# Attention and a two-layer MLP in one kernel: the first batch's queries in two token halves, PSUM banks handed out by age

## The chip, the cores and the metric

The kernel runs on one core of a Trainium2 chip. A core has five engines that run side by side, each through its own queue in order: TensorE (PE, matmuls), VectorE (DVE), ScalarE (ACT), GpSimd (POOL) and SyncE (SP, which issues loads and stores). They meet through semaphores. The metric is the device time of one execution in microseconds; a row of the profile gives times in microseconds too, from the start of the span.

## The reference

Eight batches of twelve heads, 448 tokens and 64 features per head. Queries and keys are scaled to length one, scores are divided by tau = 0.1, softmax weights are applied to the values, and the heads' outputs stand side by side as 3584 rows of 768. Those go through two matrices with a hard swish in between.

```python
q_n = q / (np.linalg.norm(q, axis=-1, keepdims=True) + 1e-06)
k_n = k / (np.linalg.norm(k, axis=-1, keepdims=True) + 1e-06)
attn = softmax(np.matmul(q_n, k_n.transpose(0, 1, 3, 2)) / tau)
x = heads_side_by_side(np.matmul(attn, v))        # 3584 x 768
h = x @ w_in                                      # 3584 x 2048
out = (h * np.clip(h + 3.0, 0.0, 6.0) / 6.0) @ w_out
```

## The kernel before

**Tiling.** Heads are taken in pairs, six pairs to a batch, 48 in all; pair i belongs to batch i // 6. A pair of heads fills the 128 partitions, 64 features each. A query or key load (`load_qk`, an "item") brings the rows of two pairs; its squares are summed (`square`, `reduce`), turned into inverse lengths (`norms` on ACT, or `powers` and `reciprocals` with DVE), and multiplied in (`normalise`). In the first 14 items `transposes` turns the result on PE into PSUM, from where `copy_q`, `copy_k` and `copy_k3` bring it to SBUF; later items are turned by a transposing DMA.

**Scores and values.** `scores(i, g)` makes the scores of group g of pair i, with the keys on the partitions. Groups 0 to 2 hold 128 keys of each head, as two matmuls on the upper and lower half of the array; group 3 holds the last 64 keys of both heads. `exps` takes the exponential on ACT (softmax needs no maximum here, since the scores are bounded), `values` multiplies with the values, which carry a column of ones so that the sums come out as a 65th column, and `finish_values` divides on DVE. `back` (or a transposing DMA) turns the result into `xT`, the first layer's input, and `copy_x` brings it to SBUF.

**Layers.** `mm1_unit(b, fc)` is one of 16 units of the first layer for a batch: six matmuls of 448 columns, a Relu on ACT and one product on DVE. The second layer's units are `mm2_unit`, and `product_unit` for pairs of row blocks that share sums of weights (`weight_sums`, `g_sum`).

**Order.** Up to pair 18 (`FIRST`) the order of all work is written out by hand in `PLAN`, a list of words that `run` reads one by one; each word appends instructions to the queue of the engine that does it. From pair 18 on a loop (L1089) interleaves attention with the units that `TURNS` names, the same for every pair of its kind. The words:

| word | work | engine |
|---|---|---|
| LQ.j, LV.d, W | load of an item, of values, of a piece of the weights | SP, SP, POOL |
| SQ.j.e, RE.j, NO.d, NM.j.e | squares, sums, inverse lengths, scaling | e, DVE, ACT, e |
| TR.j, CQ.i.e, CK.i.e, CS.i.e | transposes and copies of queries and keys | PE, e, e, e |
| SC.i.g, EX.i.g, VA.i.g, FI.i | scores, exponentials, values, division | PE, ACT, PE, DVE |
| BK.i, CX.i.e, VC.i.e | transposes back, their copy, cast of values | PE, e, e |
| U, UA, UV | a unit's matmuls, its ACT step, its DVE step | PE, ACT, DVE |
| DP.n, D.n | n fillers: matmuls of zeros of 248 or 512 columns | PE |

(e is a, v or p for ACT, DVE or POOL.) The first rows of the plan of before:

```python
"LQ.1 DP.5 SQ.1.a.11.3 SQ.1.p.4.3 DP.1 SQ.1.a.0.4 LQ.0 SQ.0.p.8.6 DP.2 DP.4 LQ.3 LQ.2 SQ.1.v.7.4 RE.1.1",
"SQ.0.a.0.6 RE.1.0 NO.0.1 LQ.5 LQ.4 SQ.0.v.6.2 DP.6 SQ.3.a.0.7 NM.1.p.0 D.10 RE.0.1 DP.3 NM.1.p.1 RE.0.0 DP.8",
"NO.0.0 LV.0 DP.2 SQ.2.a.0.7 NM.0.p.0 RE.3 RE.2 NM.0.p.1 TR.1.Y DP.2 TR.0.Z CK.0.v DP.4 SQ.4.p.0.7 CQ.0.v",
"SQ.5.a.0.7 LQ.6 NO.1 LV.1 LQ.7 SC.0.0.0 SC.0.1.1 DP.5 DP.3 CQ.1.v EX.0.0 RE.5 RE.4 NM.3.p SC.0.2.0 CK.1.v",
```

The first unit (the first U) stands in its fifteenth row, after all of batch 0's values, pair 6's exponentials and most of pair 7's.

**PSUM.** Eight banks. While batch 0 runs, four hold scores two by two (`SC`, L1078), one exponential reading both, two (`PV`) the values, and `Y` and `Z` what else is turned. After batch 0 `open_ring` (L1020) makes a ring of six single banks in a fixed order of turns. `bank_of` notes at build time how many readers a bank still has; what runs on the chip is only the waits that follow from the order.

Of the kernel before, what the change touches and what calls it, by code (L numbers as in the profile page):

```python
# [18 lines left out]
ORDER = "1111111111111111111111111111112222222122"  # L19

PLAN = [
# [43 lines left out]
def kernel(  # L65
# [61 lines left out]
    def item(n):  # L127
# [4 lines left out]
        for c in range((NR + 2) * RAW, (NR + 2) * RAW + NV * VAL, VAL)  # L132
    ]
    NVX = 4
    vx = [const.tile([128, 8, D + 1], BF16, name=f"vx{i}", tag=f"vx{i}") for i in range(NVX)]
    raws = [item((i + 2) % NR) for i in range(NR)]

    def raw_before(j):
# [21 lines left out]
    def next_bank():  # L160
        ring_n[0] += 1
        return ring[(ring_n[0] - 1) % len(ring)]
# [1032 lines left out]
```

## Time and profile before

| what | value |
|---|---|
| median of 3 runs | 402.08 us (401.6 to 402.13) |
| span of the profiled execution | 399.5 us |
| PE busy | 391.4 us, 98% of the span |
| DVE, ACT, POOL busy | 291.1, 274.3, 235.9 us |
| granted clock of PE, mean | 0.999 |
| first unit of the first layer | 39.65 us |
| first score of the loop (pair 18) | 114.67 us |

The time of the profiled execution itself is not given, only its span from the first to the last instruction; the runs' median lies 2.6 us above that. Busy time is the union of an engine's instructions. For PE it runs from a matmul's start to the end of its latency, so that a short burst shows more busy time than the array was fed for, and the distance from one start to the next tells what a matmul costs.

### The profile page before, as it was taken

To read this page: it belongs to the slowest core of one execution; us is meant where nothing else is said; L and a number is where in the kernel's file an instruction comes from. 1 tells how busy PE (TensorE), PEld (TensorE's weight loads), DVE (VectorE), ACT (ScalarE), POOL (GpSimd) and SP (SyncE) were. 2 spreads that over 40 slices of the span, in tenths; PEclk is the share of its full clock that TensorE was granted. 3 is DMA by queue.
4 is the path that set the end of the run, shared out by engine and by line. 5 is a ranking of instruction groups with operands and counts; after the bars stand their busy time and mean duration, and the time that the engine had idled before them with its cause. 6 is when DMAs were issued, how large, how long until landed. Compare 5 with 4: busy or idle time off the path is not lost.

```text
span 399.5 us, 9623 instructions
## 1 busy us (share of the span) xinstructions
PE 391.4 (98%) x3673; PEld 230.9 (58%) x3673; DVE 291.1 (73%) x514; ACT 274.3 (69%) x627; POOL 235.9 (59%) x234
## 2 busy tenths in 40 slices
PE   7999999999999999999999999999999999999996
PEld 5656466555555556555555555555565556555563
DVE  6898988889878597766878775976766565645663
ACT  6899998886887676887776776767658655224230
POOL 7897229652853989579859829688396500400070
PEclk9999999999999999999999999999999999999999
DMA  8999987797987678795888386694953424230133
GB/s 292 291 226 252 240 188 206 149 172 193 222 201 171 159 193 183 174 231 152 196 178 230 81 203 158 155 198 136 193 125 75 103 48 67 46 74 21 31 71 97
DMA packets 92365, 63.73 MB, mean 160 GB/s; under 512 B 56096, under 2 KB 91552, under 8 KB 92320
## 3 DMA queue, kind: packets, MB, share of 16 engines
q1 hardware_dynamic: 87408, 56.45, 58.6%
q0 software_dynamic: 4512, 6.29, 9.3%
q8 instruction: 28, 0.46, 0.5%
q10 hardware_dynamic: 400, 0.39, 0.3%
q14 instruction: 17, 0.14, 0.1%
HBM read 45.61 MB, written 11.01 MB: 142 GB/s over the span
## 4 chain that ended last, share of the span: by engine, by line
PE 90%; ACT 5%; DMA 1%; DVE 1%; POOL 1%; issue 0%; SPq 0%; ACTq 0%
PE M L598 24%; PE M L794 19%; PE PV L486 11%; PE Y L598 6%; PE Z L598 6%; PE M L445 5%; PE Z L794 5%; PE Y L794 4%; ACT at L463 4%; PE Z L445 1%; PE Y L445 1%; PE M L874 1%; PE PV L1016 1%; DMA big<-in_q_dram 1%; POOL nrm L297 1%; PE Z L659 1%
## 5 line engine op out<-in xcount | busy, mean ns | idle before, releaser
L598 PE MATMUL M<-xT,w_in_sb 128*128 128x448 bf16 x522 | 110.7, 353 | 0.1
L598 PEld LDWEIGHTS <-w_in_sb 128*128 128x128 bf16 x768 | 72.0, 98 | 62.2 <-issue 1.9
L463 ACT ACTIVATE at<-M 128x448 bf16<-128x448 f32 x192 | 96.4, 569 | 16.7 <-PE M L445 15.7
L297 POOL TENSOR_TENSOR nrm<-big,r 128x896 bf16<-128x896 f32 (+1 forms) x46 | 77.1, 1680 | 27.8 <-ACT r L260 10.7
L229 POOL TENSOR_TENSOR big<-big 128x896 f32<-128x896 f32 (+3 forms) x41 | 60.8, 1488 | 16.6 <-DVE n L241 11.0
L620 DVE SCALAR_TENSOR_TENSOR gT<-u,M 128x448 bf16<-128x448 bf16 x76 | 46.2, 616 | 32.0 <-ACT u L614 31.8
L614 ACT ACTIVATE u<-M 128x448 bf16<-128x448 f32 x87 | 48.5, 560 | 28.3 <-PE M L598 27.9
L486 PEld LDWEIGHTS <-at 128*128 128x128 bf16 (+1 forms) x1536 | 53.0, 97 | 22.8 <-issue 14.4
L486 PE MATMUL PV<-vx,at 128*128 128x65 bf16 (+1 forms) x1536 | 62.3, 193 | 0.3 <-DVE on L507 0.2
L241 DVE TENSOR_REDUCE n<-big 128x14 f32<-128x896 f32 (+1 forms) x50 | 51.7, 1041 | 5.7 <-POOL big L229 3.9
L794 PEld LDWEIGHTS <-gT 128*128 128x128 bf16 x336 | 32.5, 98 | 23.3 <-issue 0.4
L823 POOL TENSOR_TENSOR big<-big 128x384 f32<-128x384 f32 x13 | 13.4, 1034 | 53.7 <-ACT big L842 53.5
L794 PE MATMUL M<-w_out_sb,gT 128*128 128x384 bf16 x224 | 40.2, 326 | 0.0
L794 PEld LDWEIGHTS <-gs 128*128 128x128 bf16 x280 | 27.0, 98 | 18.7 <-issue 0.5
L402 POOL COPY km<-tT 64x128 bf16<-64x128 bf16 x34 | 14.0, 413 | 34.7 <-PE M L445 9.7
L507 DVE TENSOR_TENSOR on<-PV,rc 128x512 bf16<-128x512 f32 x48 | 33.2, 691 | 1.7
L794 PE MATMUL M<-w_sum,gs 128*128 128x384 bf16 (+1 forms) x192 | 34.2, 323 | 0.0
L463 ACT ACTIVATE at<-Y 128x448 bf16<-128x448 f32 x52 | 29.6, 569 | 6.0 <-PE Z L445 5.9
L445 PE MATMUL M<-tT,kz 64*128 64x448 bf16 x169 | 31.1, 351 | 0.3 <-DVE gT L620 0.2
L463 ACT ACTIVATE at<-Z 128x448 bf16<-128x448 f32 x50 | 28.8, 576 | 0.4 <-PE M L445 0.4
L598 PE MATMUL Y<-xT,w_in_sb 128*128 128x448 bf16 x126 | 27.4, 353 | 0.0
L316 POOL CAST vx<-big 128x512 bf16<-128x512 f32 x36 | 24.1, 672 | 4.9 <-DMA big<-in_v_dram 4.9
(137 smaller groups left out, 563.1 us busy)
## 6 DMA issues: line engine op xcount, KB each, us to landing
big<-in_k_dram SPq DMA_DIRECT2D x24, 448.0 KB, 4.5
big<-in_q_dram SPq DMA_DIRECT2D x24, 448.0 KB, 4.2
out_dram<-o SPq DMA_DIRECT2D x107, 96.0 KB, 2.2
big<-in_v_dram SPq DMA_DIRECT2D x48, 128.0 KB, 4.2
big<-in_v_dram SPq DMA_DIRECT2D x48, 96.0 KB, 4.1
w_out_sb<-in_moe_w_out_dram POOLq DMA_DIRECT2D x4, 768.0 KB, 9.4
w_in_sb<-in_moe_w_in_dram POOLq DMA_DIRECT2D x4, 384.0 KB, 10.7
w_in_sb<-in_moe_w_in_dram POOLq DMA_DIRECT2D x2, 768.0 KB, 21.5
```

The costliest lines, as they stand in the source:

```text
L229: engines[e].tensor_tensor(out=o, in0=i, in1=i, op=ALU.mult)
L241: nc.vector.tensor_reduce(out=n2s[d % 2][:, j % 2, c], in_=sq[:, :, :, :].rearrange("p g c d -> p (g c) d")[:, c, :], axis=AX.X, op=ALU.add,)
L297: engines[e].tensor_tensor(out=nrm[:, :, g, :].rearrange("p c g d -> p g c d"), in0=raw_of[j][:, g, :, :], in1=rs[d % 2][3][:, j % 2, :] . ...
L316: (engines[e].copy if e == "a" else engines[e].tensor_copy)(out=o, in_=f)
L445: nc.tensor.matmul(o, ks, qt[rows], start=True, stop=True)
L463: nc.scalar.activation(out=o, in_=x, func=AF.Exp, scale=inv_tau)
L486: nc.tensor.matmul(pv_out(j, h), at[rows, n, q_cols(i // HP, j)], vt[rows, 3 + h if name == "M" else 5 * h + int(name[1]), :], start=(name ...
L507: nc.vector.tensor_tensor(out=on[:, :, :, :].rearrange("p j h d -> p h j d"), in0=pv4[:, :, :, 0:D], in1=rc[:, :, :].to_broadcast([128, 2, ...
L598: nc.tensor.matmul(ps[:, 0:S], w_in_sb[:, cc, fc * 128 : (fc + 1) * 128], x[:, cc, 0:S], start=(cc == 0), stop=(cc == CC - 1),)
L614: nc.scalar.activation(out=u[:, :], in_=ps[:, 0:S], func=AF.Relu, bias=0.5, scale=1.0 / 6.0)
L620: nc.vector.scalar_tensor_tensor(out=g[:, fc, c0 : c0 + S], in0=u[:, :], scalar=1.0, in1=ps[:, 0:S], op0=ALU.min, op1=ALU.mult,)
L794: nc.tensor.matmul(m, lhs[:, c, :], rhs[:, c, c0 : c0 + width], start=(base is None and c == 0), stop=(c == KC - 1), skip_group_check=True,)
```

## The change

**Halves.** Batch 0's 448 tokens are taken as 256 and 192 (`span_of`). For each pair and half, `half_scores(i, h, x)` makes groups 0 and 1 (x = 0) or 2 and 3 (x = 1) in two banks, `half_exps` reads each bank with one exponential of 512, 384, 256 or 192 columns, `half_values` adds up in one bank per half (two in turn, `half_pv`), `half_finish` divides, and `half_back` and `half_copy_x` bring the half to `xT`. In x = 1 group 3 goes into a bank that group 2 writes too, so PE waits for its own matmul first (`wait`). Words hS, hE, hV, hF, hB, hX name these. All 16 first-layer units of batch 0 run twice, on 256 columns (U.f) and on 192 (U.l); U.x are whole units of batch 1, U.s the second layer's. UA and UV name the unit they finish (UA.f3), so that they need not come in order.

**Buffers of batch 0.** Keys, queries and values of batch 0 get a buffer for each pair, laid into the tiles that later hold sums of weights (`kz_first`, `qT_first`, `vx_first`).

**PSUM.** The ring of six single banks is there from the start; `bank_of` gives the bank that has been free longest. The other two hold the halves' values, then `PV`.

**Constants.** The ones and zeros of the later value buffers are cleared by POOL; DVE clears those of the first batch's five in one piece and a sixth apart, and a column range of the six exponential buffers.

**Order.** `PLAN` is written anew (its first eleven rows stand below). Fillers: 68 of 248 columns in place of 79 and ten of 512. The code of the loop stays, but for the banks.

```diff
@@ PLAN
+    "LQ.1 SQ.1.a.7.4 LQ.0 LQ.3 SQ.1.v.11.3 RE.1.1 SQ.1.a.0.4 LQ.2 SQ.1.a.4.3 RE.1.0 SQ.0.a.8.6 SQ.0.p.0.6 NO.0.1",
+    "NM.1.p.0 NM.1.p.1 DP.55 TR.1 SQ.0.v.6.2 RE.0.1 RE.0.0 SQ.3.a.0.7 NO.0.0 NM.0.p.0 RE.3 LQ.5 NM.0.v.1 SQ.2.a.0.7",
+    "RE.2 CK.0.a SQ.5.a.0.7 LV.0 VC.0.p DP.8 TR.0 CQ.0.v CK.1.v VC.1.v LQ.6 DP.4 hS.0.1.0 W LQ.4 hS.0.1.1 NO.1",
+    "hE.0.1.0 NM.3.p hS.0.0.0 CQ.1.v hS.1.0.0 hE.0.1.1 LV.2 hV.0.1.0 hE.0.0.0 hS.0.0.1 W NM.2.p W hE.0.0.1 hS.1.1.0",
+    "hV.0.1.1 hE.1.0.0 RE.5 LV.1 TR.3 hS.1.0.1 DP.1 TR.2 SQ.4.v.0.7 hV.0.0.0 hV.0.0.1 RE.4 NO.2 hF.0.1 CK.3.v",
+    "hE.1.1.0 hV.1.0.0 hS.1.1.1 CQ.2.v LQ.7 CK.2.v hE.1.0.1 hS.2.0.0 CQ.3.v NM.5.p hE.1.1.1 W W W hF.0.0 hS.3.0.1",
+    "hE.2.0.0 hV.1.0.1 hE.3.0.1 VC.3.p hS.3.0.0 NM.4.v TR.4 TR.5 VC.2.p hF.1.0 hV.1.1.0 CQ.5.v hS.2.0.1 hV.1.1.1",
+    "CQ.4.v hE.3.0.0 CK.4.v hS.4.0.0 CK.5.v hS.5.0.0 hF.1.1 hV.2.0.0 hV.3.0.0 hE.2.0.1 hV.2.0.1 SQ.7.p.0.7 VC.4.v",
+    "hV.3.0.1 VC.5.p hB.0.0 hF.2.0 SQ.6.p.0.7 hE.4.0.0 hX.0.0.v hS.4.0.1 hF.3.0 hE.5.0.0 hV.4.0.0 hS.5.0.1 RE.7",
+    "hE.4.0.1 LQ.9 hE.5.0.1 hS.4.1.1 hE.4.1.1 hB.2.0 hX.2.0.v hV.4.0.1 hF.4.0 hV.5.0.0 hB.1.0 LQ.8 hX.1.0.v hB.3.0",
+    "hV.5.0.1 hS.4.1.0 LV.3 hX.3.0.a hS.3.1.1 hE.4.1.0 hF.5.0 hB.4.0 hX.4.0.v hE.3.1.1 hB.5.0 SQ.9.p.0.7 hX.5.0.v U.f",
...
-    PV = psum.tile([128, 2, 512], FP32, name="PV", tag="PV")
-    Y = psum.tile([128, 512], FP32, name="Y", tag="Y")
-    Z = psum.tile([128, 512], FP32, name="Z", tag="Z")
-    ring = []
+    ring = [psum.tile([128, 512], FP32, name=f"M{n}", tag=f"M{n}") for n in range(6)]
+    half_pv = [psum_h.tile([128, 512], FP32, name=f"H{n}", tag=f"H{n}") for n in range(2)]
...
     def next_bank():
-        ring_n[0] += 1
-        return ring[(ring_n[0] - 1) % len(ring)]
+        one = [n for n in range(6) if free(n)]
+        return ring[min(one, key=age)]
+    def release(key):
+        unread[key] -= 1
+        if not unread[key]:
+            ring_n[0] += 1
+            freed[key] = ring_n[0]
...
+    def half_scores(i, h, x):
+        kt, qt = score_operands(i, 0)
+        q0, w = span_of(h)
+        two, keys = zip(bank_of(1), bank_of(1))
+        for s in range(2):
+            if x and s:
+                break
+            for n in range(2):
+                rows = slice(64 * n, 64 * n + 64)
+                g = 2 * x + s
+                last = nc.tensor.matmul(two[n][:, 256 * s : 256 * s + w], kt[rows, 128 * g : 128 * g + 128],
+                                        qt[rows, q0 : q0 + w], start=True, stop=True, skip_group_check=True)
+                if n == 0:
+                    upper = last
+        if x:
+            for n in (1, 0):
+                rows = slice(64 * n, 64 * n + 64)
+                if n:
+                    wait = nc.tensor.nop(nofuse=True)
+                    tc.add_manual_dep(wait.ins, upper.ins.name, info, reason="one half of the array at a time in a bank")
+                nc.tensor.matmul(two[0][rows, 256 : 256 + w], kt[rows, KM : KM + SR], qt[rows, q0 : q0 + w],
+                                 start=True, stop=True, skip_group_check=True)
...
+    def half_exps(i, h, x):
...
+        for n, z in enumerate(two):
+            src, to = (t.rearrange("p (s n) -> p s n", n=256)[:, 0 : 2 - x * n, 0:w] for t in (z[:, :], at[:, n, :]))
+            nc.scalar.activation(out=to, in_=src, func=AF.Exp, scale=inv_tau)
...
+    def mm1_unit(b, fc, ends=None, h=None):
+        needs(*(("CX", i) if h is None else ("hCX", i, h) for i in range(b * HP, (b + 1) * HP)))
+        q0, w = (0, S) if h is None else span_of(h)
...
     def busy(n):
-        bank_of("Y", 0)
+        z = next_bank()
         for _ in range(n):
-            nc.tensor.matmul(Y[:, :], zeros[:, 0:128], zeros[:, :], start=True, stop=True)
+            nc.tensor.matmul(z[:, 0:248], zeros[:, 0:128], zeros[:, 0:248], start=True, stop=True)
...
-    for t in vx:
-        nc.vector.memset(t[:, :, D : D + 1], 1.0)
...
+    for t in (five, vx_first[5].rearrange("p (i c) d -> p i c d", i=1)):
+        nc.vector.memset(t[:, :, :, D : D + 1], 1.0)
...
+    for t in vx:
+        nc.gpsimd.memset(t[:, :, D : D + 1], 1.0)
...
+    for t in ats[2]:
+        nc.vector.memset(t[:, :, 192:256], 1.0)
```

More of the change, by code (lines that the diff above doesn't have):

```diff
@@ new lines, in half_exps @@
+    def half_exps(i, h, x):
+        at = ats[2][at_n[2] % len(ats[2])]
+        assert all(x is not at for x in at_of.values()) and (i, h, x) in sc_of
+        at_n[2] += 1
+        at_of[(i, h, x)] = at
+        w = span_of(h)[1]
+        two, keys = sc_of.pop((i, h, x))
+        for key in keys:
+            release(key)
+        for n, z in enumerate(two):
+            src, to = (t.rearrange("p (s n) -> p s n", n=256)[:, 0 : 2 - x * n, 0:w] for t in (z[:, :], at[:, n, :]))
+            nc.scalar.activation(out=to, in_=src, func=AF.Exp, scale=inv_tau)
@@ new lines, with half_values @@
+    pv_n, half_n = [0], [0]
+    pv_of, half_on, half_tiles = {}, {}, []
+    def half_values(i, h, x):
+        needs(("VC", i), ("hE", i, h, x))
+        if x == 0:
+            assert not pv_of.get(pv_n[0] % 2)
+            pv_of[i, h] = pv_n[0] % 2
+            pv_of[pv_n[0] % 2] = True
+            pv_n[0] += 1
+        else:
+            needs(("hV", i, h, 0))
+        bank = pv_of[i, h]
+        at = at_of.pop((i, h, x))
+        vt = vx_of(i)
+        parts = [(0, 0, 0), (0, 1, 1), (1, 0, 5), (1, 1, 6)] if x == 0 else [(0, 0, 2), (1, 0, 7), (0, 1, 3), (0, 1, 4)]
+        for y, (n, s, c) in enumerate(parts):
+            head = int(c > 3)
+            for j in range(2):
+                nc.tensor.matmul(
+                    half_pv[bank][:, (D + 1) * (2 * head + j) : (D + 1) * (2 * head + j + 1)],
+                    at[:, n, 256 * s + 128 * j : 256 * s + 128 * j + 128],
+                    vt[:, c, :],
+                    start=(x == 0 and y == 0 and j == 0),
+                    stop=(x == 1),
+                    skip_group_check=True,
+                )
+        if x:
+            issued.add(("hVA", i, h))
+            if ("hVA", i, 1 - h) in issued:
+                issued.update(("VA", i, g) for g in range(4))
@@ new lines, in half_back, with half_copy_x @@
+    def half_back(i, h):
+        needs(("hF", i, h))
+        z, key = bank_of(1)
+        z = z.bitcast(BF16)
+        z_of[-1 - i, h] = z, key
+        for j in range(2):
+            nc.tensor.transpose(z[:, 128 * j : 128 * j + 128], half_on[i, h][1][:, j, :, :], ident[:, :])
+    def half_copy_x(i, h, e="v"):
+        z, key = z_of.pop((-1 - i, h))
+        release(key)
+        q0, w = span_of(h)
+        copy(e, xT[0][:, i, q0 : q0 + w], z[:, 0:w].rearrange("p (t n) -> p t n", n=64))
+        issued.add(("hCX", i, h))
+        if ("hCX", i, 1 - h) in issued:
+            issued.update((("BK", i), ("CX", i)))
@@ L512, in finish_values, with back @@
         )
-    def back(i, bank=None):
-        z, key = bank_of(bank, 1)
-        if bank is not None:
-            z = z[:, :].bitcast(BF16)
+    def back(i):
+        needs(("FI", i))
+        z, key = bank_of(1)
         z_of[-1 - i] = z, key
```

276 lines of the change are left out of this document (178 added, 98 removed), and 72 rows, old and new, of the table PLAN.

## The prediction

> **What bounds the kernel now.** I read the page first: one engine, PE, is busy nearly throughout, and its clock is granted in full.
>
> ```profile
> span 399.5 us, 9623 instructions
> PE 391.4 (98%) x3673; PEld 230.9 (58%) x3673; DVE 291.1 (73%) x514; ACT 274.3 (69%) x627; POOL 235.9 (59%) x234
> ```
>
> The table by stretches comes next, cut at the first first-layer unit (39.65) and at the first score of the loop (114.67):
>
> ```profile
> 0.00:39.65 39.65, 35.82 (x447) 23.75 (x447) 32.69 (x82) 34.11 (x69) 32.75 (x45) 1.00 0.99 265
> 39.65:62.50 22.85, 22.57 (x244) 12.89 (x242) 19.87 (x37) 21.74 (x53) 7.65 (x6) 1.00 0.97 221
> 62.50:114.67 52.17, 52.09 (x504) 29.70 (x501) 44.33 (x76) 42.88 (x101) 30.99 (x32) 1.00 0.89 189
> 114.67:399.50 284.83, 280.88 (x2491) 164.59 (x2488) 194.23 (x322) 175.60 (x409) 164.56 (x153) 1.00 0.59 135
> ```
>
> From 39.65 on PE is full, so what counts is how much PE work stands there and when the full stretch begins. Ahead of 39.65 PE's 35.82 is not what it seems: it holds fillers and the tails of short bursts. PE's timeline and, for back-to-back prices, the chain of waits (there a piece runs to the next one's start) give the durations:
>
> ```profile
> 2.48 3.89 PE L1016 MATMUL PV<-xT 128*128 128x248 bf16 x18 [2.48 <-DVE vx L1067]
> 6.17 2.36 PE L1011 MATMUL Y<-xT 128*128 128x512 bf16 x10
> 8.37 1.54 PE L1016 MATMUL PV<-xT 128*128 128x248 bf16 x13
> 9.74 0.55 PE L342 MATMUL Y<-ident,nrm 128*128 128x128 bf16 x7
> 21.38 0.36 PE L445 MATMUL SC<-tT,kz 64*128 64x448 bf16 x2
> 21.68 0.42 PE L486 MATMUL PV<-vx,at 128*128 128x65 bf16 x8
> 22.16 0.38 PE L442 MATMUL SC<-tT,kz 64*64 64x448 bf16 x2
> 22.46 0.42 PE L486 MATMUL PV<-vx,at 128*128 128x65 bf16 x8
> 39.65 0.54 PE L598 MATMUL M<-xT,w_in_sb 128*128 128x448 bf16 x2
> 114.67 0.36 PE L445 MATMUL Z<-tT,kz 64*128 64x448 bf16 x1
> ```
> ```profile
> 59.95 1.14 PE Y L598 x6
> ...
> 63.84 0.19 PE M L445
> 64.03 0.39 PE M L342 x7
> 64.42 0.24 PE PV L486 x8
> ...
> 113.19 1.30 PE Y L794 x8
> ```
>
> Prices: a filler 0.205 while the array is cold ((6.17 - 2.48)/18) and 0.105 warm ((9.74 - 8.37)/13), the wide one 0.22; a unit 1.14, so 0.19 for 448 columns and 0.42 per 1000; seven transposes 0.39; a pair of scores 0.30; the split fourth group 0.30; a whole one 0.19; a value group 0.24-0.25; eight products 1.30. By the plan's order, before, ahead of the first unit: 71 + 10 fillers (9.7), 9 transposes (3.5), 24 + 6 + 2 score groups (9.4), 27 value groups (6.7), 6 transposes back (1.3): 30.6. With the first 2.48 and the cold surcharge (18 x 0.1) that is 34.9; PE stood 4.8 us. Behind: 31 units, 5 transposes, 30 pairs, 10 whole groups, 42 value groups, 8 fillers, 4 transposes back, two second-layer units and seven products: 74.7. It took 114.67 - 39.65 = 75.0, so this pricing is 0.3 us short over 75.
>
> What ends the waiting ahead of 39.65 is ACT: 34.11 busy of 39.65, and back to back once exps run:
>
> ```profile
> 4.31 0.67 ACT L227 ACTIVATE big<-big 128x192 f32<-128x192 f32 x2 [2.29 <-DMA big<-in_k_dram]
> 8.69 1.77 ACT L227 ACTIVATE big<-big 128x896 f32<-128x896 f32 x2
> 12.20 2.54 ACT L463 ACTIVATE at<-SC 128x896 bf16<-128x896 f32 x3 [0.42 <-PE SC L445]
> 14.61 0.24 ACT L257 ACTIVATE ln<-n 128x28 f32<-128x28 f32 x1
> 15.58 2.26 ACT L463 ACTIVATE at<-SC 128x448 bf16<-128x448 f32 x3
> 17.73 0.95 ACT L227 ACTIVATE big<-big 128x896 f32<-128x896 f32 x1
> 20.38 2.97 ACT L463 ACTIVATE at<-SC 128x896 bf16<-128x896 f32 x4 [0.46 <-PE SC L445]
> 38.23 1.52 ACT L463 ACTIVATE at<-M 128x448 bf16<-128x448 f32 x3
> 39.50 0.69 ACT L463 ACTIVATE at<-Y 128x448 bf16<-128x448 f32 x1
> ```
>
> Three exps of 896 columns take 14.61 - 12.20 = 2.41 (0.80 each), three of 448 take 39.50 - 38.23 = 1.27 (0.42): 0.84 per 1000 columns and about 0.05 per instruction. Four norm steps take 15.58 - 14.61 = 0.97.
>
> **The change, part by part.**
>
> *First unit earlier.* The first batch's exps run by token halves, and U.f0 needs only the first halves of six pairs. First the front. 55 fillers stand ahead of TR.1: 2.48 + 18 x 0.205 + 37 x 0.105 = 10.1, against 9.74 now. On ACT come the square (from 8.69 to about 9.6), then CK.0, now on ACT, which waits for the transposes (10.1 + 0.55) and ends about 11.1, a square (0.84) and NO.1 (0.97): the first half exp starts at 13.0, against 12.20, 0.8 later. Up to the one that U.f0 needs, hE.5.0.1, there are 16 half groups, 32 instructions and 13,440 columns: 13.44 x 0.84 + 32 x 0.05 = 12.9; with NO.2 0.97 and 0.6 of idle, as ACT has now between 12.20 and the first unit (0.46 of it in the row at 20.38), it ends at 27.5. Behind it stand eight value matmuls, hF, two transposes, hX. DVE's rows price hF:
>
> ```profile
> 4.32 0.42 DVE L229 TENSOR_TENSOR big<-big 128x256 f32<-128x256 f32 x1 [0.84 <-DMA big<-in_k_dram]
> 43.66 1.15 DVE L620 SCALAR_TENSOR_TENSOR gT<-u,M 128x448 bf16<-128x448 bf16 x2
> 44.73 0.20 DVE L506 RECIPROCAL rc<-PV 128x8 f32<-128x8 f32 x1
> 44.97 0.69 DVE L507 TENSOR_TENSOR on<-PV,rc 128x512 bf16<-128x512 f32 x1
> 45.57 0.17 DVE L284 TENSOR_SCALAR le<-nr 128x28 f32<-128x28 f32 x1
> ```
>
> FI takes 45.57 - 44.73 = 0.84, a half about 0.6 (the reciprocal as long, half of the rest); values 0.4 with their tail, transposes 0.3, copy 0.4, and 0.3 for hands between engines: 2.0. First unit: 29.5, 10.1 us earlier than now.
>
> *PE's work.* After, ahead of the first unit: 68 fillers (7.2), 6 transposes, 16 half value groups, 6 half transposes, and 19 half score groups. A half score group has matmuls of 256 or 192 columns (0.108, 0.081) and 0.1 for changing over, as in the pair (0.30 - 0.19): 0.32 and 0.26. The second kind also holds a wait of PE for its own matmul; no row shows one. Ends: 0 where PE stands for ACT anyway, 0.36 (that matmul's own row) where it does not, so 0 to 12 x 0.36 = 4.3 us in all; I take 0.25, as the matmul is shorter. So 0.54 and 0.49, and 22.1 in all. Ten of the twelve waits stand ahead of the first unit, under ACT. Behind it: 16 + 16 half units (0.65, 0.49: together one whole), 15 whole units, 36 pairs, 12 whole groups, 53 value groups of both kinds, 8 transposes, 5 remaining half score groups, 6 half and 4 whole transposes back, and the same two second-layer units and seven products: 82.3. So 7.6 us of PE work moves from ahead of the first unit to behind it, and the unit comes 10.1 earlier.
>
> *Load behind the first unit.* The same pricing of ACT's queue there gives 72.8 after against 62.2 before, where the windows show 21.74 + 42.88 = 64.6 of 75.0 (86%): 92% of 82.3 after. DVE: 75.9 against 67.2 priced, 64.2 shown: 88%. Whole-batch products stay 0.53 each (the two at 43.66), halves add about 0.06 each. That ACT at 95% (21.74 of 22.85) left PE 99% busy in the second window shows the load can be borne; I add 0.5 for stalls to the 0.3 above.
>
> *PSUM, constants, loads.* Banks by age change who waits for whom, not how many: six serve the ring now, and six after; in the loop PE is busy 280.88 of 284.83, the rest is the end, so nothing is gained or lost there. The clears that leave DVE cost nothing: DVE waits 0.84 for the first load after them; on POOL they lie ahead of its first data work, which waits for the queries' load. The weight loads, all six of the first layer's, move ahead:
>
> ```profile
> 24.32 0.85 POOL L1004 DMA_DIRECT2D w_in_sb<-in_moe_w_in_dram  x1
> 26.83 2.67 POOL L1004 DMA_DIRECT2D w_in_sb<-in_moe_w_in_dram  x4
> 12.76 1.69 POOL L297 TENSOR_TENSOR nrm<-big,r 128x896 bf16<-128x896 f32 x1
> DMA to landing us min/median/max: 5.8/13.9/23.6
> ```
>
> On POOL one issue stands ahead of each of NM.3, NM.2 and NM.5 (1.69 each; NM.3 from 13.0, after NO.1) and three behind them: 13.0 + 3 x 1.69 + 2 x 0.85 + 2.5, the sixth at about 22. NM.2 and NM.5, whose transposes PE's queue waits for, come 0.85 and 1.7 later for it, at 17.2 and 19.8; in that time PE waits for exps anyway. SP's queue issues fewer key and query loads before 25 us than now, since LQ.9 waits for NM.2. At the median of 13.9 the sixth lands at 36, and U.f8, the first to need it, comes at about 40 (29.5 + 10.7 of PE work).
>
> *Sum.* Loop from 29.5 + 82.3 + 0.3 + 0.5 = 112.6 against 114.67: 2.1 earlier, rounded to 2.0. What lies behind is the same 284.8, so the span goes from 399.5 to 397.5. The median of the runs, 402.08, is 2.6 above this span; I keep that: **400.1**.
>
> **The rivals.**
>
> 1. *Dearer small exps.* ACT sets the first unit; with 0.09 instead of 0.05 per instruction 32 x 0.04 = 1.3 more, and 401.4, within 0.2%. For it: no exp of fewer than 448 columns is in the trace; against: 896 and 448 fit one line. The Trainium skill, page "ScalarE: Activation LUTs", section "What ACT_TABLE_LOAD costs", has 186 ns + 0.833 per element with 93 ns of overlap, that is 93 ns per further instruction. By that rule the sum is this rival's; the trace agrees with its 0.83 per element, and shows the smaller constant.
> 2. *The third weight piece is late* (the other side). At the longest landing, 23.6, from 22 it is there at 45.6, and PE, which takes its queue in order, stands from 40: 5.6 lost, 3.6 over the gain: 405.7. It decides from a landing 20 us after its issue. For it: DMA share is 0.99 in the first window. Against: six issues within 6 us made those landings long; here they spread over ten.
> 3. *Banks.* Each half score group holds two of six ring banks until both exps have read, while units want one; before, the first batch's scores had four banks of their own. If PE stalls 4 us more in the 27 us up to the last half unit: 404.1. Against it stands the second window.
> 4. *A cold array.* Only 13 fillers remain after the 55. At half rate the 13 us of PE work up to the first unit would take 26, 8 us later: 408. Rows show 1.00 in every stretch, with a few fillers from 20 on. The Trainium skill, page "TensorE: Matmul & The Clock Gate", Part 1, puts the drop at an idle window of about 3.4 us; the trace agrees on the warm-up (3.7 us of cold fillers), and I find no idle of that length in the order.
>
> **How the numbers follow.** 0.2% (0.8 us) is about what can be told from no change. Forecast 0.56; a better case in which the half groups' waits hide wholly and the first unit comes at 28, 398.6, 0.06; rival 1 0.13; rival 2 0.09; rival 3 0.13; rival 4 0.03. Faster 0.62, same 0.13, slower 0.25. The range leaves out rivals 2 and 4 and a little at each end: 397.5 to 404.2; the forecast's own is 398.9 to 401.2 (first unit 29.1 to 30.1, stalls behind it 0 to 1.3).
>
> **What would show it.** After: first unit at 29 to 30.5, fillers 68, first half exp at 13.0, exps of 512 columns 0.48 apart; loop's first score at 111.8 to 113.5; PE busy over 98% between. A first unit beyond 31, PE idle before `w_in_sb` matmuls of the ninth unit, or gaps before scores that ACT releases would make it wrong.

## The result

| what | before | after |
|---|---|---|
| median of the runs | 401.86 us (401.6 to 402.13, 4 runs) | 407.90 us (405.8 to 410.84, 4 runs) |
| ratio, with its 95% interval | | 1.015 (1.0103 to 1.0196) |
| profiled execution: span | 399.5 us | 404.0 us (its time 405.8) |
| first unit | 39.65 us | 29.59 us |
| loop's first score | 114.67 us | 118.96 us |
| granted clock, each execution | 0.999 (profiled) | 0.999, 0.996, 0.996, 0.992 |

The change made the kernel slower by 1.5%. Ratios, here and below, leave out executions more than 1.5% above the fastest of their kernel, which flatters versions with many of them; medians and clocks are those of all executions.

The page of the changed kernel, and its table by stretches, cut at the first unit, at the sixteenth half unit on 256 columns (52.50), and at the loop's first score. A stretch's row gives its length, the busy time (and instructions) of PE, PE's weight loads, DVE, ACT and POOL, the granted clock, the DMA share and GB/s.

```profile
span 404.0 us, 9994 instructions
PE 390.9 (97%) x3796; PEld 238.5 (59%) x3796; DVE 298.7 (74%) x538; ACT 275.4 (68%) x674; POOL 245.1 (61%) x249
```
```profile
0.00:29.59 29.59, 25.90 (x327) 18.80 (x327) 23.82 (x65) 24.08 (x62) 24.55 (x49) 1.00 1.04 268
29.59:52.50 22.91, 19.37 (x259) 15.13 (x257) 20.59 (x46) 17.84 (x56) 16.43 (x13) 1.00 1.11 256
52.50:118.96 66.46, 64.96 (x727) 41.02 (x727) 58.41 (x109) 58.37 (x151) 40.11 (x37) 1.00 0.93 183
118.96:404.00 285.04, 280.69 (x2489) 163.50 (x2488) 195.92 (x319) 175.15 (x407) 164.03 (x152) 1.00 0.57 133
```

The first unit stands where it was forecast and the loop is as long as before (285.04 against 284.83). The loss lies between: PE is idle 3.5 of the 22.9 us behind the first unit, where the stretch of before that answers to it had 0.3. ACT is at 78% there, less than before (95%); DVE is at 90%, and POOL went from 7.65 of 22.85 to 16.43 of 22.91.

PE's timeline names the waits (in brackets: idle time and what ended it):

```profile
42.47 0.82 PE L774 MATMUL M<-xT,w_in_sb 128*128 128x256 bf16 x6 [1.17 <-DMA w_in_sb<-in_moe_w_in_dram]
47.16 0.81 PE L774 MATMUL M<-xT,w_in_sb 128*128 128x256 bf16 x6 [1.62 <-ACT tT L408]
52.50 0.81 PE L774 MATMUL M<-xT,w_in_sb 128*128 128x256 bf16 x6 [0.45 <-DVE gT L796]
104.19 0.35 PE L490 MATMUL M<-tT,kz 64*128 64x448 bf16 x1 [0.48 <-DVE gT L796]
```

The first is the ninth unit, waiting for the third piece of the weights. The second is the twelfth unit, waiting for a bank, and its cause stands on three other engines:

```profile
42.00 4.25 DVE L274 TENSOR_TENSOR big<-big 128x896 f32<-128x896 f32 x1
46.17 0.38 DVE L410 COPY tT<-M 128x448 bf16<-128x448 bf16 x1
41.94 1.70 POOL L274 TENSOR_TENSOR big<-big 128x896 f32<-128x896 f32 x1
43.58 1.70 POOL L342 TENSOR_TENSOR nrm<-big,r 128x896 bf16<-128x896 f32 x1
46.58 0.53 ACT L408 COPY tT<-M 128x448 bf16<-128x448 bf16 x1 [1.71 <-DVE tT L410]
```

A square that DVE does in 1.09 us elsewhere (at 101.26) took 4.25. It began 0.06 us after POOL had begun a square of its own (41.94), and ended 0.97 us after POOL's second operation had (43.58 + 1.70 = 45.28). Behind it in DVE's queue stands CQ.9.v, which empties a bank; ACT's CQ.8.a follows at 46.58, and then PE goes on.

By the prediction's prices PE's work behind the first unit is 82.3 us; the stretch took 118.96 - 29.59 = 89.4, which is 7.1 more (some expectations below speak of 7.0 and take all of it for stalls). For 5.0 of them PE stood idle (3.5 and 1.5 by the two rows of the table): 1.17 for the weights, 1.62 for the bank, 0.45 at 52.50 (run 8), 0.66 around 104, and the rest in pieces of under 0.4. The other 2.0 are work that took longer than priced: PE was busy for 84.3.

### The profile page after: what moved, and what is told of

Read it like the earlier page. It is cut to its first block, busy times and chain, and to the rows that moved or that the text cites. A ratio compares the mean times of both kernels' runs of the same rounds, so it can differ in the third digit from the quotient of the medians.

```text
span 404.0 us, 9994 instructions
## 1 busy us (share of the span) xinstructions
PE 390.9 (97%) x3796; PEld 238.5 (59%) x3796; DVE 298.7 (74%) x538; ACT 275.4 (68%) x674; POOL 245.1 (61%) x249
## 4 chain that ended last, share of the span: by engine, by line
PE 75%; DMA 6%; DVE 5%; POOL 4%; ACT 4%; issue 3%; SPq 2%; POOLq 0%; ACTq 0%
PE M L774 27%; PE M L973 27%; PE PV L664 8%; PE M L490 5%; DMA big<-in_v_dram 4%; PE M L1190 2%; POOL nrm L342 2%; PE M L530 1%; DMA big<-in_k_dram 1%; DVE big L274 1%; PE M L1053 1%; PE H L588 1%; ACT at L508 1%; POOL big L274 1%; ACT u L790 1%
## 5 line engine op out<-in xcount | busy, mean ns | idle before, releaser
L774 PE MATMUL M<-xT,w_in_sb 128*128 128x448 bf16 (+2 forms) x864 | 165.6, 332 | 3.5 <-ACT tT L408 1.6
L508 ACT ACTIVATE at<-M 128x448 bf16<-128x448 f32 x294 | 141.3, 567 | 24.0 <-PE M L490 23.4
L796 DVE SCALAR_TENSOR_TENSOR gT<-u,M 128x448 bf16<-128x448 bf16 (+2 forms) x128 | 69.8, 558 | 45.0 <-ACT u L790 44.4
L790 ACT ACTIVATE u<-M 128x448 bf16<-128x448 f32 (+2 forms) x144 | 74.3, 523 | 41.0 <-PE M L774 40.2
L274 POOL TENSOR_TENSOR big<-big 128x896 f32<-128x896 f32 (+2 forms) x39 | 62.0, 1594 | 11.5 <-DVE n L286 4.8
L973 PE MATMUL M<-w_out_sb,gT 128*128 128x384 bf16 x336 | 60.8, 326 | 0.0
L973 PE MATMUL M<-w_sum,gs 128*128 128x384 bf16 (+1 forms) x272 | 48.0, 321 | 0.2 <-DVE big L1030 0.2
L490 PE MATMUL M<-tT,kz 64*128 64x448 bf16 (+1 forms) x260 | 38.3, 351 | 1.4 <-DVE gT L796 0.7
L951 DVE TENSOR_TENSOR gT<-gT 128x1024 bf16<-128x1024 bf16 x21 | 21.9, 1044 | 0.6
L951 DVE TENSOR_TENSOR gs<-gT 128x1024 bf16<-128x1024 bf16 x27 | 21.3, 796 | 0.0
```

The source lines that it names most:

```text
L274: engines[e].tensor_tensor(out=o, in0=i, in1=i, op=ALU.mult)
L490: nc.tensor.matmul(o, ks, qt[rows], start=True, stop=True)
L508: nc.scalar.activation(out=at[:, n, 0:S], in_=x, func=AF.Exp, scale=inv_tau)
L774: nc.tensor.matmul(ps[:, 0:w], w_in_sb[:, cc, fc * 128 : (fc + 1) * 128], x[:, cc, q0 : q0 + w], start=(cc == 0), stop=(cc == CC - 1),)
L790: nc.scalar.activation(out=u[:, 0:w], in_=ps[:, 0:w], func=AF.Relu, bias=0.5, scale=1.0 / 6.0)
L796: nc.vector.scalar_tensor_tensor(out=g[:, fc, c0 + q0 : c0 + q0 + w], in0=u[:, 0:w], scalar=1.0, in1=ps[:, 0:w], op0=ALU.min, op1=ALU.mult,)
```

## The experiments

Theories: A, DVE is held off while POOL works on SBUF; B, the weights land too late; C, too few fillers at the start lower the clock; D, small loads are late further on; E, PE's own waiting lowers the clock; F, late first loads make some executions long. All edits are to words of `PLAN` unless told. "Loop" is the loop's first score in the profiled execution.

**1. The long square on ACT.**

```diff
-SQ.10.v.0.7
+SQ.10.a.0.7
```


> One square moves from VectorE to ScalarE: the one that took 4.25 us at 42.00 while GpSimd ran two operations of its own (1.70 us each), where the same operation alone takes about 1.09. Theory A (VectorE's square is held off while GpSimd works on SBUF, and what is queued behind it holds back TensorE): the wait of 1.62 us ahead of the first-layer unit at 47.16 goes, the loop's first score comes at about 117.4 in place of 118.96, and the ratio to the kernel before falls by about 0.004 (1.5 us). Theory B (the late weights set the pace there, and the long square only fills a hole): the wait moves to another cause, the loop's first score stays within 0.3 us of 118.96 and the ratio at 1.015.

Measured: 406.39 us, ratio 1.0102 (1.0057 to 1.0146), loop 117.84. PE's waits:

```profile
42.44 0.81 PE L774 MATMUL M<-xT,w_in_sb 128*128 128x256 bf16 x6 [1.39 <-DMA w_in_sb<-in_moe_w_in_dram]
46.14 0.81 PE L774 MATMUL M<-xT,w_in_sb 128*128 128x256 bf16 x6 [0.64 <-ACT tT L408]
```

The bank's wait fell from 1.62 to 0.64 (ACT now does the square ahead of its copy), and the loop came 1.1 us earlier, 0.3 of it already at the first unit (29.33). A holds; 0.4 less than expected.

**2. No third piece.**

```diff
-nc.gpsimd.dma_start(out=o, in_=w)
+if len(weights) not in (4, 5): nc.gpsimd.dma_start(out=o, in_=w)
...
-w_in_sb[:, cc, fc * 128 : (fc + 1) * 128],
+w_in_sb[:, cc, fc % 8 * 128 : (fc % 8 + 1) * 128],
```


> The third piece of the first layer's weights (two loads of 768 KB) is left out, and the units that would read it read the first and second pieces again, so what the first layer gives is another thing; all other work stays. Theory B (late weights): the wait of 1.17 us at 42.47 goes, other loads land earlier, and the loop's first score comes 1.2 to 2.5 us earlier than 118.96. Theory A (VectorE held off by GpSimd): the wait at 42.47 goes, but the one at 47.16 grows by what was won, so that the loop's first score moves by less than 0.4 us.

Measured: 407.32 us, ratio 1.0123 (1.0075 to 1.0171), loop 119.63. The ninth unit no longer waits; the twelfth does, longer:

```profile
47.31 0.81 PE L774 MATMUL M<-xT,w_in_sb 128*128 128x256 bf16 x6 [2.93 <-ACT tT L408]
```

The two waits were 2.79 us together and this one is 2.93, so B alone is worth nothing while the bank is held: the late weights cover a part of what the held square costs. And this wait was dearer than itself, so that the loop's first score holds more than waits:

```profile
44.73:48.15 3.42, 0.84 (x13) 0.77 (x13) 3.42 (x5) 1.42 (x4) 1.09 (x2) 1.00 1.12 245
48.15:51.56 3.41, 3.41 (x25) 2.43 (x22) 2.36 (x5) 1.86 (x6) 3.36 (x3) 0.50 1.16 231
```

The granted clock is 0.50 for the 3.41 us behind it. This led to theory E.

**3. Twenty more fillers between 13 and 29 us** (ten `DP.2`, one of them a `DP.1` made `DP.3`).

```diff
-hE.0.1.0 NM.3.p hS.0.0.0 CQ.1.v
+hE.0.1.0 NM.3.p hS.0.0.0 DP.2 CQ.1.v
...
-TR.3 hS.1.0.1 DP.1 TR.2
+TR.3 hS.1.0.1 DP.3 TR.2
```


> Twenty filler matmuls are added between 13 and 29 us, in ten pairs, where TensorE is 70 to 90% busy. Theory C (the runs differ because the granted clock falls in some of them, 0.992 to 0.999, as TensorE is not busy enough at the start): every run shows 0.998 or more, the spread of the runs falls from 5.0 to under 1.5 us, and the median comes to about 406 (ratio 1.010). If the clock has another cause: clocks from 0.992 to 0.999 as before, and a median of 408 to 409, the fillers costing up to 1 us.

Measured: 410.58 us, ratio 1.0114 (1.0071 to 1.0157); clocks 1.0, 1.0, 0.99, 0.987; loop 120.30. C falls: the clock still fell in half of the executions. In the profiled one the first unit came at 31.01, the ninth unit found its weights, and the twelfth waited for the bank as in 2; but here the clock stayed at 1.00 (run 8 tells why).

```profile
48.58 0.81 PE L774 MATMUL M<-xT,w_in_sb 128*128 128x256 bf16 x6 [2.95 <-ACT tT L408]
```

**4. A key load ahead of two transposing DMAs.**

```diff
-XD.16 LQ.20 UA.s2
+XD.16 UA.s2
...
-LQ.19 U.x UA.x2
+LQ.19 LQ.20 U.x UA.x2
```


> One key load that was issued at 95.92 behind two transposing DMAs, and landed 5.3 us later, is issued right behind the load before it (about 87). Theory D (late small loads hold VectorE's queue in the second half of the stretch ahead of the loop): VectorE's wait of 1.20 us ahead of the square at 101.26 goes, TensorE's stalls at 104.2 and 105.1 (1.15 us together) go, the loop's first score comes 0.6 to 1.1 us earlier. Otherwise: VectorE's wait goes and TensorE's stalls stay within 0.3 us, since a bank or ScalarE is late there.

Measured: 405.78 us, ratio 1.0081 (1.0047 to 1.0116). The waits at 104 and 105 are gone from PE's timeline, so D holds there. The loop's first score is no measure here (120.17): in this execution the ninth unit waited 1.96 us, 3.41 us at half clock followed, and PE stood 1.55 us more at 72.75 for a reason that the profile doesn't show.

```profile
40.70:44.11 3.41, 1.45 (x12) 0.72 (x10) 3.34 (x6) 1.30 (x4) 3.41 (x4) 1.00 1.09 287
44.11:47.52 3.41, 3.41 (x24) 2.19 (x22) 3.41 (x4) 1.98 (x5) 1.08 (x2) 0.50 1.12 241
```

**5. Banks first** (with the edit of 4).

```diff
-SQ.10.v.0.7 CQ.9.v RE.10 LQ.12 CQ.8.a LQ.13 U.f
+CQ.9.v LQ.12 CQ.8.a SQ.10.v.0.7 RE.10 LQ.13 U.f
```


> Two edits: the long square of VectorE is put behind the two copies that empty the banks (it was ahead of them), and the key load of the run before stays early. Theory A (a held-off VectorE delays the bank): the square may still take 4 us, but the unit that waited 1.62 us at 47.16 waits under 0.5, and TensorE is 1.1 to 1.6 us earlier at the loop's first score than with the key load alone. The unit at 42.5 still waits 1.2 to 2.0 us for the third piece, so that the granted clock still falls in some runs (0.996 or less): ratio about 1.005, spread over 3 us. If the square only fills a hole, the wait stays over 1.2 us under another name.

Measured: 404.43 us, ratio 1.0075 (1.0011 to 1.0138), loop 116.60, clocks 1.0, 1.0, 0.999, 0.994. The bank's wait is gone. DVE and POOL met the other way round:

```profile
41.74 1.08 DVE L274 TENSOR_TENSOR big<-big 128x896 f32<-128x896 f32 x1
```
```profile
41.79 2.57 POOL L274 TENSOR_TENSOR big<-big 128x896 f32<-128x896 f32 x1 [0.32 <-DMA big<-in_k_dram]
```

DVE began 0.05 us earlier and took its usual 1.08; POOL, which needs 1.68 to 1.70, took 2.57. So no square was held here, and the new order was not tried against a held one; run 6 does that.

**6. Weights in four quarters** (with 4 and 5; two `W` more, in a row with the others).

```diff
-PIECES = [slice(0, d_ff // 4), slice(d_ff // 4, d_ff // 2), slice(d_ff // 2, d_ff)]
+PIECES = [slice(f * d_ff // 4, (f + 1) * d_ff // 4) for f in range(4)]
```


> As the run before, and the first layer's weights come in four quarters of two loads of 384 KB each in place of two quarters and a half (two loads more, 1.4 us more of issuing on GpSimd), so that the ninth unit needs only the third quarter. Theory B (late weights) with theory E (a long wait of TensorE there lowers the clock to half for the 3.41 us that follow): the third quarter lands before 37, the wait at 42.5 goes, every run shows 0.998 or more, the spread falls under 2 us, and the ratio comes to 1.000 to 1.003. If the DMA queues as a whole are the limit, the fourth quarter or the value and key loads are late instead, and a stall of over 1 us stands between 43 and 60.

Measured: 405.75 us, ratio 1.0083 (1.0039 to 1.0126), loop 117.38, clocks 0.999, 0.999, 0.998, 0.995. No unit waits for weights any more, but the square met POOL again (3.95 us). The bank's copy stands ahead of it now; DVE's products stand behind it, and a score waited for those: no gain, as in 2.

```profile
47.81 0.35 PE L490 MATMUL M<-tT,kz 128*128 128x448 bf16 x1 [2.53 <-DVE gT L796]
```

**7. Fillers where the ninth unit waits** (`DP.14` ahead of it, in the changed kernel).

> The changed kernel as it is, with fourteen filler matmuls (1.5 us of TensorE) in the place where the ninth unit waits for its weights. No load lands earlier. Theory E (it is TensorE's own waiting that lowers the clock): the clock stays at 0.998 or more in all runs, the spread falls from 5 to under 2 us, and the median falls to 405.5 to 406.5 although work was added. If the clock falls for another reason: clocks of 0.992 to 0.996 in two or three of four runs as before, and a median of 408 or more.

Measured: 407.83 us, ratio 1.0114 (1.0041 to 1.0187), clocks 0.999, 0.998, 0.992, 0.990. A miss: filling this one wait does not keep the clock up. In the profiled execution the bank's wait is gone too, though nothing else was changed: beside the same two operations of POOL the square took 2.61, and POOL's second operation was the one that waited.

```profile
42.12 2.61 DVE L274 TENSOR_TENSOR big<-big 128x896 f32<-128x896 f32 x1
```
```profile
43.73 2.56 POOL L342 TENSOR_TENSOR nrm<-big,r 128x896 bf16<-128x896 f32 x1
```

**8. Quarters, and `NO.5` in place of `NA.5 ND.5`.**

> As the run with quarters, and one small operation of VectorE on SBUF that took 0.77 us in place of 0.17 while GpSimd worked (51.04), with the reciprocal behind it, is done by two small activations of ScalarE instead. Theory A: the wait of 0.45 us at 52.50 goes and the loop's first score comes 0.3 to 0.6 us earlier than with quarters alone. Otherwise it stays within 0.2 us, or comes later by the two activations (some 0.5 us of ScalarE).

Measured: 407.73 us, ratio 1.0109 (1.0048 to 1.017). The wait for DVE at the sixteenth half unit fell from 0.59 (in 6) to 0.26; what that brings at the loop can't be read, since a half-clock stretch stands ahead of it. Beside 6, this run shows what decides about the clock: in both, one score waited 2.53 us. First the two stretches of 6, then those of 8:

```profile
43.10:46.51 3.41, 2.19 (x30) 1.57 (x27) 3.38 (x2) 2.47 (x7) 2.25 (x2) 1.00 1.12 266
46.51:49.93 3.42, 2.12 (x27) 1.87 (x27) 3.42 (x7) 1.46 (x5) 2.42 (x2) 1.00 1.14 239
```
```profile
45.62:49.03 3.41, 0.90 (x14) 0.75 (x13) 3.38 (x4) 1.23 (x4) 1.25 (x2) 1.00 1.15 232
49.03:52.45 3.42, 3.39 (x19) 2.37 (x19) 2.38 (x5) 1.43 (x4) 3.40 (x3) 0.50 1.14 244
```

The stretches are steps of 3.41 us, counted from where the clock first rose. In 6 the wait fell across two steps, and the clock stayed; in 8 it lay within one, and the next step ran at half. The waits of 2 (2.93, within one) and 3 (2.95, across two: PE busy 2.21 and 1.66) go the same way.

**9. All of it** (4, 5, 6, 8, and `SQ.10.a` behind `CQ.8.a`).

> The run with quarters and without the reciprocal, and the long square goes to ScalarE behind the copy that empties the bank, so that neither VectorE nor a bank waits for GpSimd in this stretch, and no unit waits for the third piece. Theories A, B and E together: no wait of TensorE over 0.7 us between 40 and 53, the loop's first score at 115.5 to 116.3, the clock at 0.998 or more in most runs, a ratio of 0.998 to 1.003. If the stalls only move from one late thing to the next: a new wait of over 1 us, loop's first score at 117 or later, ratio 1.006 or more.

Measured: 403.84 us over 12 executions, ratio 1.0018 (0.9991 to 1.0045), nine clocks at 0.998 or more, three at 0.983 to 0.992 (these three are not in the ratio); loop 117.55. A wait of 1.09 us for DVE stays at 47.30 (DVE's products behind a sum that waits for ACT's square), and the first unit came at 30.57, 1.0 later than in the changed kernel; so the loop is 1.3 us later than hoped.

**10. One GpSimd operation less beside the square** (`SQ.11.a` in place of `SQ.11.p`, in the changed kernel).

> In the changed kernel one of the two GpSimd operations that ran beside VectorE's square of 4.25 us (the square of 1.70 us) goes to ScalarE; VectorE's own square stays where it is. Theory A, by the arithmetic of a VectorE that starts only when GpSimd's operation has ended: one operation of 1.70 us and then its own 0.9 to 1.1, so at most 2.8 us in place of 4.25, and 1.1 if it comes first. If the 4.25 us come from a late load or from the memory of that square's tile, they stay over 3.5 us.

```profile
47.36 2.62 DVE L274 TENSOR_TENSOR big<-big 128x896 f32<-128x896 f32 x1
```
```profile
47.31 1.70 POOL L342 TENSOR_TENSOR nrm<-big,r 128x896 bf16<-128x896 f32 x1
```

2.62 in place of 4.25: one operation of POOL less, 1.63 us less. That is A's arithmetic. The run's time, 410.25 us, says nothing on the edit: its first values landed at 13.5 in place of 11.3, DVE's next square waited 1.68 us for a query load and took 2.87 beside POOL, PE waited 0.9, 1.6 and 0.3 us between 18 and 23, and the clock was 0.50 from 20.58 to 27.41.

**11. The sixth weight load later.**

```diff
-hE.1.1.1 W W W hF.0.0
+hE.1.1.1 W W hF.0.0
...
-SQ.6.p.0.7 hE.4.0.0
+SQ.6.p.0.7 W hE.4.0.0
```


> In the changed kernel the sixth load of the first layer's weights is issued some 5 us later on GpSimd, so that the ninth unit waits longer for it; nothing else changes. Theory E (a wait of TensorE of 2 us and more lowers the granted clock to half for the next 3.41 us): wait at the ninth unit of 3 to 6 us, a stretch of half clock of 3.41 us right behind it, and a clock of 0.996 or less in every one of the runs; the time grows by the longer wait and 1.7 us more, to 410 to 413. If the clock has another cause: some runs at 0.999 as before, and the time grows by the wait alone or by less.

Measured: 411.79 us, ratio 1.014 (1.0067 to 1.0213), clocks 1.0, 0.995, 0.988, 0.977. A miss in its own terms: one execution kept its clock, and in the profiled one the front was late like that of 10 (half clock from 16.93 to 30.59), so that the ninth unit found its weights. There the twelfth unit waited 2.94 us for the bank, and the next 3.41 us ran at half.

**12. A value load later** (9, with `LV.2` behind `LQ.7`, and the two added `W` behind `VC.2.p`).

> The run with all stalls mended, with one value load (four DMAs, 3.3 us of SP) moved behind the next query load, and the two added weight issues of GpSimd moved behind a value cast that TensorE waited 0.66 us for at 24.9. Theory F (the slow executions come from the first loads: a query load issued beside eight value DMAs lands 4 us late in some executions, VectorE's square then meets GpSimd's operations, TensorE waits some 3 us between 17 and 22 and its clock falls): of eight or more executions at most one shows a clock under 0.995, where three of twelve did, and the fast ones come to 402.0 to 403.5 (ratio 0.998 to 1.002). If the late loads have another cause: as many executions over 408 as before, and the same ratio within 0.002.

Measured: 403.40 us, ratio 1.0016 (0.9996 to 1.0036), loop 116.14. Four of twelve clocks were 0.987 to 0.992, so this load is not F's cause.

**13. The sum behind the products** (12, with `RE.10` behind `UV.f10`).

> The run before with one sum of VectorE put behind the products of two units; in the run before the sum waited 2.48 us for ScalarE's square, and TensorE waited 1.09 us for the products queued behind it. If stalls of this kind are what is left of the 7.0 us: that wait goes, the loop's first score comes 0.8 to 1.1 us earlier (115.0 to 115.4), and the ratio falls by 0.002 to 0.999. If another late thing stands right behind it: under 0.4 us earlier and the same ratio within 0.001.

Measured: 404.01 us, ratio 1.0031 (1.0005 to 1.0057), loop 115.57. The wait of 1.09 is gone. First unit to loop it is now 86.1 us, as in 12 (86.0): a score waits 0.75 for a copy at 88.17 instead. The second outcome, where it counts.

**14. A query load ahead of the first value load** (13, with `LQ.4` ahead of `LV.0`).

> As the run with the sum behind the products, with the query load that was late in the two slow fronts put ahead of the first value load (0.5 us of SP). Theory F, the other half: its lateness makes VectorE's square meet GpSimd's operations and TensorE wait; then at most one of eight or more executions has a clock under 0.995, where seven of twenty-four had. If what comes late at the front is any load, by chance: as many clocks under 0.995 as before, and the first values and the first unit 0.3 to 0.5 us later.

Measured: 407.14 us, ratio 1.0118 (1.0097 to 1.0139), all four clocks 0.992. It went the other way and so made the late front at will: the first values were cast at 12.95 in place of 11.45, DVE's next square met two operations of POOL, and PE waited for a division that stands behind it.

```profile
14.90 4.47 DVE L274 TENSOR_TENSOR big<-big 128x896 f32<-128x896 f32 x1
```
```profile
21.10 0.60 PE L588 MATMUL H<-w_sum,at 128*128 128x65 bf16 x8 [1.57 <-DVE on L615]
```
```profile
17.42:20.83 3.41, 1.51 (x26) 1.06 (x25) 3.34 (x4) 0.40 (x3) 1.63 (x2) 1.00 1.21 225
20.83:27.66 6.83, 6.03 (x56) 3.85 (x55) 5.32 (x14) 5.59 (x15) 5.93 (x8) 0.50 1.14 256
```

The first unit came at 34.73 in place of 29.50: one load 0.5 us later on SP cost 5.2 us.

**15. That square on ACT** (13, with `SQ.4.a`).

> The run with the sum behind the products, with the square of the fifth load at the front (1.32 us on VectorE in undisturbed fronts; 2.87, 2.96 and 4.47 us beside GpSimd in the three profiled late fronts) moved to ScalarE, which pays 0.95 us in the stretch that sets the first unit. Theory A at the front: it is this square meeting GpSimd that makes fronts late and the clock fall. Then no execution has a clock under 0.995 (seven of twenty-four had), the first unit stands at 30 to 30.6 in place of 29.5, and the ratio is 1.000 to 1.004 with a spread under 3 us. If the late first loads do it without the square: as many clocks under 0.995 as before.

Measured: 406.64 us, ratio 1.0089 (1.006 to 1.0118); eight of ten clocks 0.989 to 0.994, first unit 34.02. A miss: the meeting with POOL is not needed. ACT does the square only at 17.43, behind ten exponentials; the sum behind it starts at 18.44, where 13 has 16.01 and 14 has 19.41, and the division follows it.

**16. The first value load ahead of a key load** (13, with `LV.0` ahead of `LQ.5`).

> The run with the sum behind the products, with the first value load ahead of one key load (0.5 us earlier on SP; the key load 2.7 us later). In the late fronts the first value cast began at 12.95 to 14.46, in the others at 11.16 to 11.65. If it is the values' landing that tips the front: at most one of eight or more clocks under 0.995 and the fast ones as in the run before, 401.6 to 403.5. If the key load's lateness matters more: ScalarE waits for it, the first unit comes after 30, and as many clocks under 0.995 as before or more.

Measured: 402.74 us over 12 executions, ratio 0.9986 (0.996 to 1.0011), loop 115.69; two clocks under 0.995. The best version, level with the kernel before.

**17. The key load of 4 behind a value load** (16, with `LQ.20` behind `LV.9`).

> The run with the value load first, with the key load of the earlier run now behind the next value load instead of ahead of it, so that fewer loads stand beside the transposing DMA that a score waits 1.09 us for at 88.28 (0.39 in the changed kernel). If that load is what delays it: the wait falls to 0.4 or less, the loop's first score comes 0.5 to 0.7 us earlier than 115.69, and the ratio falls by 0.001 to 0.002, to 0.997. If the eight value DMAs delay it: no change.

Measured: 403.53 us, ratio 1.0047 (1.0018 to 1.0077). The wait is gone, and first unit to loop is 85.5 us (16: 86.4), so the load of 4 had given a part of its gain back. But five of twelve clocks are 0.995 or less, so 16's better clocks are not shown to come from its edit.

**18. The division ahead of the sum** (16, with two words moved and the square given to ACT).

```diff
-SQ.4.v.0.7 hV.0.0.0 hV.0.0.1 RE.4 NO.2 hF.0.1 CK.3.v hE.1.1.0
+SQ.4.a.0.7 hV.0.0.0 hV.0.0.1 hF.0.1 RE.4 CK.3.v hE.1.1.0 NO.2
```


> The run with the value load first, with three words moved at the front: the square goes to ScalarE, the first half's division goes ahead of the sum in VectorE's queue, and the inverse lengths go behind two more exponentials. In both fronts that were late in nearly every execution (the square of 4.47 us beside GpSimd; the square on ScalarE) TensorE waited 1.3 to 1.6 us for that division at 20 to 21, and half clock followed. Theory A carried over to the front (what tips it is the division queued behind a late sum): at most one of twelve clocks under 0.995, median 402 to 403, ratio 0.997 to 1.002. If the inverse lengths or the exponentials behind them are what comes late: clocks of 0.992 as in the run with the square on ScalarE, and a first unit beyond 32.

Measured: 405.46 us, ratio 1.008 (1.005 to 1.0111), clocks 0.989 to 0.999, first unit 31.38. The wait for the division is gone and half clock fell from two steps to one, but it came all the same:

```profile
12.25:15.66 3.41, 2.68 (x31) 1.18 (x26) 1.88 (x3) 3.31 (x11) 2.45 (x3) 1.00 1.10 294
15.66:19.07 3.41, 3.27 (x35) 2.49 (x33) 1.65 (x4) 3.10 (x7) 2.21 (x2) 0.50 1.18 254
```

What the front needs for a steady clock stays open.

## Why the prediction was wrong

Forecast 400.1, measured 407.9. In the profiled execution the loop's first score came 6.4 us later than forecast (118.96 against 112.6), nearly all of it behind the first unit (89.4 in place of 83.1); what lies around its span was 1.8 in place of 2.6; the median lies 2.1 above that execution.

- *First unit earlier*: right, 29.59 against 29.5; the first half exp began at 13.20 and exps of 512 columns start 0.48 apart, so rival 1 (dearer small exps) is out. But it is a front with no slack: first values cast 1.5 us later made it 34.73 (run 14), a sum 2.4 us later 34.02 (run 15).
- *PE's work*: 2.0 short. PE was busy for 84.3 us behind the first unit, where I priced 82.3. Run 17 says the same: with no wait of PE over 0.31 us left, the stretch still takes 85.5, with PE busy for 83.95. So 3.9 of the 89.4 went with the stalls, and 2.4 more than the forecast's 83.1 stay. Half units and changes between smaller groups may be the dear ones; I had priced changes only within half score groups. That was not worked out.

```profile
30.05:115.53 85.48, 83.95 (x986) 55.99 (x984) 73.87 (x151) 77.19 (x209) 56.84 (x50) 1.00 0.99 210
```
- *The loop unchanged*: right, 285.04 against 284.83.
- *Load behind the first unit*: this step failed. That ACT at 95% left PE 99% busy "shows the load can be borne" looked at ACT and DVE alone and gave 0.8 for all that isn't priced work; PE stood idle for 5.0. ACT was not the limit: it was busy for 76.2 of the 89.4 us (85%), less than the 92% forecast. POOL's load doubled between 29.59 and 52.50, and DVE's squares, with two SBUF operands, do not keep their 1.09 us beside it. Run 10 shows the price of one operation of POOL, run 1 that the bank's wait hangs on the square; in run 5 that wait is gone with the copy ahead of the square, and in run 6 a held square makes the products behind it late instead. The sign stood in the trace of before, in a square beside POOL's casts, and I did not read it:

```profile
38.44 1.16 POOL L316 CAST vx<-big 128x512 bf16<-128x512 f32 x2
```
```profile
38.99 1.55 DVE L229 TENSOR_TENSOR big<-big 128x896 f32<-128x896 f32 x1
```

  The Trainium skill, page "SBUF — State Buffer", section "Who interferes with whom", says that a VectorE instruction with two SBUF inputs contends with a GpSimd instruction that reads SBUF, and that the order of issue decides which of two blocks. The trace agrees in both directions (4.25 for DVE, 2.57 for POOL in run 5).
- *PSUM, constants, loads*: the landing failed. The sixth load was issued at 21.4 and landed at 42.3, 20.9 us later and not 13.9 (below, the three last issues and the landings of all six). Rival 2 said that it decides from 20; it made a wait of 1.17. "Here they spread over ten" spoke for faster landings, but the DMA share was 1.04 and 1.11 in the first two stretches, and 0.99 before. Run 2 shows that taking the load away alone gains nothing.

```profile
20.10 2.01 POOL L1183 DMA_DIRECT2D w_in_sb<-in_moe_w_in_dram  x3
DMA to landing us min/median/max: 7.6/11.1/20.9
```
- *Rival 3* named the place (units wanting banks) and the wrong holder: not the half scores, but a bank that a copy in DVE's queue should have emptied.
- *Rival 4* was right in kind and sized as a cold array throughout. By their clocks (span times what is missing from 1, an estimate) the four executions lose 0.4, 1.6, 1.6 and 3.3 us. "I find no idle of that length" asked for 3.4 us of idle; run 4 shows the clock falling after a wait of 1.96, and run 18 after a step with PE 79% busy.

So of the 7.8 us, 4.2 are idle time of PE behind the first unit (5.0 in place of 0.8), 2.0 are work there that was priced too low, and 2.1 are the median above the profiled execution, more than half of it clock by the estimate above. First unit and loop add 0.3, and 0.8 less lies around the span.

## What to carry to other kernels

Read engines that share a resource together: look for operations whose duration depends on what another engine does at the time, and put what TensorE waits for ahead of them in the queue: what empties a PSUM bank, and the products too (run 6). Work moved earlier meets loads that were issued for later; take their landings at the DMA share that the new order makes. One stall can hide the next, so a mended cause may show no gain until the other is mended too.

## What the runs showed of the hardware

- **A DVE operation can wait through two of POOL's.** The square of 1.09 us took 2.62 beside one operation of POOL, and 3.95 to 4.47 beside two in eight squares of eight executions: DVE did not get its turn between them. In run 7, beside the same two, it did (2.61), and POOL's second took 2.56. What decides the turn stays open. A small operation waits as well: adding a constant to 128x28 (0.17 elsewhere) took 0.77 in the changed kernel, and 1.30 in run 5.

```profile
51.04 0.77 DVE L329 TENSOR_SCALAR le<-nr 128x28 f32<-128x28 f32 x1
```

- **The clock goes by steps of 3.41 us.** Behind the first unit, over all twenty profiled executions, each step in which PE was busy for 0.48, 0.84, 0.90 or 1.45 us was followed by one at half clock, and none in which it was busy for 1.66 or more (1.79 in the changed kernel, from 44.40). So a wait of 2 to 3 us costs 1.7 us more (half of a step) or nothing, by where it falls. The Trainium skill, page "TensorE: Matmul & The Clock Gate", Part 1, has a free-running window of 3413 ns, and the trace's steps have that length; it lets the clock fall after an idle window, where here a step with PE busy for 1.45 us was idle enough. In the front busy time alone does not decide: steps with 1.98 (run 10), 2.68 (run 18) and 2.79 us busy (run 11) were followed by half clock, and steps with 2.49 (run 11) and 2.60 (run 6) were not. Matmuls there use 64 rows of the array and stand in short bursts, which may be why; that was not tried.
